# An attention block with an MLP: where row maxima are placed, who copies the sums, who normalizes the output rows, and how far maxima run ahead

## The chip, the core and the metric

The kernel runs on one core of a Trainium2 chip. The core has five engines that run side by side and meet only at semaphores: TensorE (PE in the profile, with its weight loads as PEld), VectorE (DVE), ScalarE (ACT), GpSimd (POOL) and SyncE (SP), which here only issues DMAs. Each engine takes its instructions strictly in the order in which they stand in its queue, so an instruction that waits holds up all that stand behind it. Matmul results land in PSUM, which has eight banks of 128 x 512 floats; everything else lies in SBUF or in DRAM. The metric is the device time of one execution in microseconds (us).

## The reference

Two pre-norm layers on a sequence of 2048 rows of 512 numbers, all in float32:

```
h  = x + softmax(q k^T / 4) v @ wo      with q, k, v = layernorm(x) @ wqkv, 32 heads of 16 columns
h2 = h + silu(layernorm(h) @ w1) @ w2   with 1792 hidden columns
```

The softmax is the exact one: each row's maximum over all 2048 keys is subtracted before the exponential.

## The kernel before

**Numbers.** Operands of most products are split into a high and a low half-precision part and multiplied in three products (high x high, low x high, high x low). Probabilities and values are multiplied in float32.

**Items and groups.** The attention works through 32 items; an item is one block of 512 query rows and four heads (`ITEMS`, eight items to a block of rows). An item has 16 groups; a group takes one chunk of 128 keys for the four heads. So there are 512 groups, g = 0 to 511, and c = g mod 16 is the place of a group in its item. A group consists of four score matmuls (`scores`, L469), four exponentials on ScalarE (`pt`, L480) and, one or two groups later, four matmuls of probabilities with values (`values`, L883), which add into one PSUM bank, `pv`, over the 16 groups of an item. A column of ones in the values gives the sums of the softmax.

**Maxima.** The exponent needs the row maximum before the scores are taken. So the scores are computed a second time, ahead: one matmul of 128 queries by 512 keys and one VectorE reduction (`maximum`, L292; the lines L308, and L306 where two heads go in one reduction). An item has 64 of these reductions. `maxima(g)` (L1376) says how many are done beside group g. When an item's last one is done (`found_maxima`, L405), `finish_max` folds them to 16 numbers on GpSimd and splits them into two half-precision rows (`ns`), and then one of two ways brings them into the query operand `qs` as two extra rows. `place_far` (L345) transposes on VectorE (`mt`), writes to DRAM (four DMAs, `md<-mt`) and reads back (two DMAs, `qs<-md`); it is called CALM groups later, or WAIT steps later before the attention starts. `place_max` (L358) transposes on TensorE, copies on VectorE (`mn`) and writes with two DMAs; it is for items that are found FAR groups or fewer before they start, and in that case GpSimd's folding is replaced by one VectorE reduction.

**Before the attention.** Layer norm, weight splits and projections run in a prologue of about 110 us, in blocks b = 0 to 3 of 512 rows. Beside each projection a few maxima of items 0 and 1 are done in pairs (`burst`). Which keys of item 0 may be used is in `at["loaded"]` (L772). After the blocks come three more query and key projections, and then group 0.

**Products beside groups.** In most groups the other work of TensorE is mixed in (`beside_products`, L1190): further query and key projections beside groups 0 to 115, and the MLP of the previous block of rows beside groups 146 to 257, 274 to 385 and 402 to 511. In such a group `maxima` gives four reductions, and five as long as fewer than 64 + 4 (g + LEAD) are done, though never past the end of the item that is being worked on. The groups between, 116 to 145, 258 to 273 and 386 to 401, have no product beside them. There the number comes from a rate that reaches the next items in time: four at most, three in many. These are the first item of a block and a little before and after it (`FIRSTS` = items 8, 16, 24; before item 8 also twelve groups of item 7).

**Output of a block.** In items 8, 16 and 24, groups c = 9 to 14, the previous block's attention output is projected with wo, four row tiles one after the other (`output`, L1236): in step n (c = 9 + n) TensorE's 12 matmuls and the sum with x of tile n, the split of tile n-2 into halves (`split_normal`, ScalarE's copy, then GpSimd's or for the last tile VectorE's subtraction), the layer norm of tile n-1 on VectorE (`normalize`, `hx<-ot`), and the statistics of tile n.

**End of an item.** `finish_item` (L901) copies `pv` to SBUF (`pvs`), the left half on ScalarE and the right half on VectorE, and starts the DMAs for the sums and the outputs. The last item's copy is followed by a tail of about 90 us, the last block's output and MLP.

**Order.** The engines' queues follow the order in which the program emits the instructions, with a few DMAs on SyncE interleaved differently where a memory pool is exchanged at group 124. Work for later is kept in an agenda by step, a step being a projection of the prologue or a group.

Of the kernel before, what the change touches and what calls it, by code (L numbers as in the profile page):

```python
# [10 lines left out]
F32 = mybir.dt.float32  # L11
# [3 lines left out]
AF = mybir.ActivationFunctionType  # L15
ALU = mybir.AluOpType
# [4 lines left out]
P = 128  # L21
# [43 lines left out]

WAIT = 2
AHEAD = 6
FAR = 8
CALM = 4


OUTPUT = 8

LOOK = 5

LEAD = 9


SWAP = 124
# [11 lines left out]
def attention_mlp_kernel(ctx: ExitStack, tc: tile.TileContext, x, wqkv, wo, w1, w2, out):  # L91
# [12 lines left out]
    def pool(op, *a, **k):  # L104
        tc.keep_in_program_order(getattr(nc.gpsimd, op)(*a, **k))  # L105
# [5 lines left out]
    def act(fn, *a, **k):  # L111
        ins = getattr(nc.scalar, fn)(*a, **k)  # L112
        pin(ins)
        return ins
# [6 lines left out]
    def dve(fn, *a, **k):  # L121
        pin(getattr(nc.vector, fn)(*a, **k))  # L122
# [110 lines left out]

    def normalize(dst, rows, mv, rs, engine="dve"):
        (pool if engine == "pool" else dve)("tensor_scalar", dst, rows, mv[:, 0:1], rs, op0=ALU.subtract, op1=ALU.mult)

    def turn(src, dst_h, dst_l, kind="st"):

# [142 lines left out]
    def soon(steps, fn, *a):  # L381

        agenda.setdefault(at["step"] + steps, []).append((fn, a))
# [21 lines left out]
    def found_maxima(piece):  # L405
        g = at["group"]
        if g is None or piece[1] is None and start_of(piece) - g > FAR:
            soon(WAIT if g is None else CALM, place_far, piece)
            finish_max(piece, False)
            return  # L410
        late.setdefault(at["step"] + WAIT, []).append(piece)
        unfinished.append(piece)
        found_at["step"] = at["step"]
# [348 lines left out]
    for b in range(NB):  # L762
        if b == 1:
            lay_out(sm=range(4), st=(7, 4, 5, 6))
        if b == NB - 1:
            lay_out(sm=range(6), st=[n for n in banks["st"] if n > 5])
        units = [("qk", 1, b), ("qk", 0, b) if b < 2 else ("qk", 3, b - 1)]
        vs = [("v", t, b) for t in range(4)]
        found = {}
        for n, (kind, k, of) in enumerate(units + vs if b else units):  # L770
            tick()
            at["loaded"] = b + (n > 3)  # L772
            square_rest(2 + 6 * (b - 1) + n if b else n)
            rows, (stats, norm, turns) = None, ((), (), ())
            if b + 1 < NB:
                rows = xts[b + 1]
                stats, norm, turns = (other_ln if b else first_ln)[n]
                if b == 2 and n < 4:
                    stats, norm = (((0, 1), (0,)), ((), (1,)), ((3,), (2,)), ((), ()))[n]

            def layer_norm():
                for of_norm in (kind == "v", kind != "v"):
                    for t in norm if of_norm else stats:
                        if of_norm:
                            normalize(rows[:, t, :], rows[:, t, :], *found.pop(t), engine="pool" if kind == "v" and (b, n) != (1, 2) else "dve")
                        else:
                            found[t] = statistics(rows[:, t, :], LN)

            if kind == "v":
                project_v(b, k)  # L790
            else:

                if (b, n) == (0, 1):
                    load_x(3)
                    for c in range(2):
                        pool("tensor_scalar", scaled[1 - c], raw_v[:, 2 + c], v_w, 1.0, op0=ALU.mult, op1=ALU.mult)
                    split_qk(splits.pop((b, n)))
                layer_norm()
                if (b, n) == (1, 0):
                    split_values(0)  # L800
                project_qk(of, k, scale=b > 0)
                if (b, n) == (0, 1):
                    split_values(1)
                if (b, n) in splits:
                    split_qk(splits.pop((b, n)))
                if n == 1:
                    for i in range(2):
                        for h in range(4):
                            if b == 0:
                                load_q(i, h)  # L810
                            load_k(i, h, b * 512, 512)
            if b:

                burst(BESIDE_V[b - 1][kind == "v"][n - 2 if kind == "v" else n])
            if (b, n) == (2, 0):
                stats, norm = (2,), ()
            if kind == "v" or (b, n) == (2, 0):
                layer_norm()
            if (b, n) == (2, 2):
                normalize(rows[:, 3, :], rows[:, 3, :], *found.pop(3), engine="pool")  # L820
            for t in turns:
                turn_x(b + 1, t)
            if b == NB - 1 and n < DC:
                split_x0(n)
            if (b, n) in splits:
                split_qk(splits.pop((b, n)), "pool")
            if b == 2 and n in (3, 5):
                fixed_rows(n // 4)
# [72 lines left out]
    def finish_item(i):  # L901

        b, u = divmod(i, 8)
        pvs = bp.tile([P, 512], F32, name="pvs", bufs=1)
        act("copy", pvs[:, :256], pv[:, :256])
        dve("tensor_copy", pvs[:, 256:], pv[:, 256:])
        if i == LAST:
            last.append(pvs)
            return
        dma(dn[i], pvs.rearrange("(k r) n -> k r n", r=32)[:, DH, :])  # L910
        for k in range(4):
            dma(ot[b % 2][place(i, k), :, u // 2, :], pvs[32 * k:32 * k + 16, :].rearrange("d (t n) -> d t n", n=P))

        steps = (1, 3, 4, 6) if u == 7 else (2, 6, 8, 10)
        for n, fn in zip(steps, (sums, invert, spread, divide) if u % 2 else (sums, invert, spread)):
            soon(n, fn, i)
        if i == ITEMS - 2:
            soon(10, divide_half)
            soon(12, split_half)
# [141 lines left out]
    def rows_of(b, t):  # L1061
        return ot[b % 2][:, t].rearrange("p c n -> p (c n)")
# [173 lines left out]
    def output(b, n):  # L1236

        if n < 4:
            ps = bank()
            run(project_rows(n, ps))  # L1240
            add_rows(b, n, ps)
        t = n - 3
        if t in halves:
            turn_beside(hts, slice(t * P, (t + 1) * P), halves.pop(t))
        t = n - 2
        if 0 <= t < 4:
            split_normal(t)
            if t == 3:
                turn_beside(hts, slice(t * P, (t + 1) * P), halves.pop(t))
        if 0 < n < 5:  # L1250
            normalize(hx[n - 1], rows_of(b, n - 1), *found.pop(n - 1))

        if n < 4:
            found[n] = statistics(rows_of(b, n), LN)
# [121 lines left out]
    def maxima(g):  # L1376
# [17 lines left out]
        at["due"] += rate  # L1394
        if g < LAG:
            return 0
        n = max(0, min(most, int(at["due"]), ready - at["done"]))
        at["due"] = min(4, at["due"] - n)
        return n
# [126 lines left out]
```

## Time and profile before

| | |
|---|---|
| median of three runs | 1618.02 us (1617.33 to 1620.47) |
| the profiled execution | 1617.63 us, of which the span from first to last instruction is 1615.9 us |
| PE busy | 1579.4 us, 98% |
| VectorE busy | 1380.6 us, 85%; 1211.8 of them 1956 reductions of single maxima |
| ScalarE busy | 1241.9 us, 77%; 1068.2 of them 2048 exponentials |
| GpSimd busy | 580.2 us, 36% |
| mean granted TensorE clock | 0.996 |

PE's busy time is no measure of how full PE is, since matmuls overlap; what counts is the distance from one group to the next. Rows of a timeline give the start and the time taken by a run of like instructions (x4 means four), and in square brackets how long the engine had been idle before it and what it waited for. The chain of waits gives the pieces of work that set the end, in order of time. In a row of stretches, an engine's busy time is followed by its number of instructions in brackets, and the columns after POOL are the granted TensorE clock, the DMA share and GB/s.

### The profile page before, as it was taken

What the parts mean: (1) busy time and instruction counts of PE and PEld (TensorE: products, weight loads), DVE (VectorE), ACT (ScalarE), POOL (GpSimd) and SP (SyncE); (2) the same over time, 40 slices, a digit from 0 to 9 for tenths busy, and PEclk for the clock granted to TensorE, in tenths of its full rate; (3) what the DMA queues carried; (4) which work ended last, traced back from release to release, by engine and by line L of the source; (5) the groups of instructions that cost most, each with busy time, mean ns of one, the idle gap of its engine ahead of it and who ended that gap; (6) DMA issues with size and microseconds to landing.
All of it is one profiled execution on the core that took longest, in us unless ns stands there. A gap on an engine that the chain in (4) does not pass through costs nothing.

```text
span 1615.9 us, 31905 instructions
## 1 busy us (share of the span) xinstructions
PE 1579.4 (98%) x11735; PEld 488.3 (30%) x11735; DVE 1380.6 (85%) x2279; ACT 1241.9 (77%) x2412; POOL 580.2 (36%) x875
## 2 busy tenths in 40 slices
PE   9979999999999999999999999999999999999999
PEld 6422233333222222222222222222222222222354
DVE  7979999999988999999989999999989999991232
ACT  5548988888876888877777888877767888878632
POOL 6631255645522444412143445311143444311100
PEclk9989999999999999999999999999999999999999
DMA  6653334444433122344424222444433122434322
GB/s 219 163 139 95 106 84 125 131 122 131 126 77 84 43 59 59 90 142 144 117 57 96 51 50 53 118 136 124 114 93 66 45 59 59 119 103 139 121 84 74
DMA packets 135993, 162.23 MB, mean 100 GB/s; under 512 B 43248, under 2 KB 79856, under 8 KB 135836
## 3 DMA queue, kind: packets, MB, share of 16 engines
q1 hardware_dynamic: 133388, 155.86, 34.6%
q10 hardware_dynamic: 2448, 4.33, 1.0%
q8 instruction: 92, 1.51, 0.4%
q14 instruction: 65, 0.53, 0.1%
HBM read 126.71 MB, written 24.85 MB: 94 GB/s over the span
## 4 chain that ended last, share of the span: by engine, by line
PE 83%; DVE 9%; ACT 3%; POOL 2%; issue 2%; DMA 1%; SPq 0%; POOLq 0%; ACTq 0%
PE ps L98 82%; DVE mx L308 6%; ACT pt L112 2%; DVE mx L306 1%; DVE pvs L122 1%; POOL w L105 1%; ACT pvs L112 1%; PE ps L101 1%; DVE st L122 0%; DVE hx L122 0%; SPq L128 0%; DMA qs<-md 0%; POOL sl L105 0%; DMA ot<-in_A_wo_dram 0%; ACT sh L112 0%
## 5 line engine op out<-in xcount | busy, mean ns | idle before, releaser
L308 DVE TENSOR_REDUCE mx<-ps 128x1 f32<-128x512 f32 x1956 | 1211.8, 682 | 72.8 <-PE ps L98 68.2
L112 ACT ACTIVATE pt<-ps 128x512 f32<-128x512 f32 x2048 | 1068.2, 604 | 252.7 <-PE ps L98 247.7
L98 PE MATMUL ps<-qs,ks 64*128 64x512 f16 x2048 | 736.6, 380 | 10.1 <-DMA qs<-md 8.8
L98 PE MATMUL ps<-ks,qs 48*128 48x512 f16 x2048 | 675.2, 380 | 19.0 <-DVE mx L308 10.7
L98 PE MATMUL ps<-pt,va 128*17 128x512 f32 x4096 | 545.1, 598 | 0.0
L98 PE MATMUL ps<-hts,w 64*128 64x512 f16 (+2 forms) x1212 | 285.7, 370 | 0.0
L98 PEld LDWEIGHTS <-qs 48*128 48x128 f16 x2048 | 156.6, 94 | 388.1 <-issue 367.7
L98 PE MATMUL ps<-w,gates 64*128 64x512 f16 x1008 | 246.4, 376 | 0.6
L98 PEld LDWEIGHTS <-ks 64*128 64x128 f16 x2048 | 186.4, 94 | 97.7 <-issue 86.1
L105 POOL TENSOR_TENSOR ri<-rc,minus 128x16 f32<-128x16 f32 x31 | 90.8, 2928 | 195.2 <-DMA rc<-dn 195.2
L98 PEld LDWEIGHTS <-w 64*128 64x128 f16 (+1 forms) x1212 | 114.4, 95 | 134.1 <-issue 36.8
L98 PEld LDWEIGHTS ps<-pt,va 128*17 128x17 f32 x4096 | 73.7, 95 | 222.6 <-issue 218.8
L98 PEld LDWEIGHTS <-gates 64*128 64x128 f16 x1008 | 92.8, 94 | 132.0 <-issue 32.0
L105 POOL TENSOR_SCALAR t<-t,factors 128x512 f32<-128x512 f32 x42 | 29.0, 691 | 187.1 <-ACT t L112 187.1
L112 ACT ACTIVATE g<-ps,factors 128x512 f32<-128x512 f32 x68 | 47.3, 696 | 43.7 <-PE ps L98 42.7
L105 POOL TENSOR_TENSOR sl<-scaled,sh 128x512 f16<-128x512 f32 x30 | 34.7, 1156 | 127.3 <-ACT sh L112 117.5
L98 PE MATMUL ps<-xth,wqk_h 64*128 64x512 f16 (+1 forms) x204 | 77.8, 382 | 0.0
L98 PE MATMUL ps<-xth,wqk_l 64*128 64x512 f16 (+1 forms) x204 | 77.7, 381 | 0.0
L98 PE MATMUL ps<-xtl,wqk_h 64*128 64x512 f16 (+1 forms) x204 | 77.5, 380 | 0.0
L105 POOL TENSOR_TENSOR ot<-ot,g 128x512 f32<-128x512 f32 x12 | 15.2, 1266 | 172.9 <-ACT g L112 172.9
L122 DVE COPY pvs<-ps 128x256 f32<-128x256 f32 (+1 forms) x33 | 14.3, 432 | 56.2 <-ACT pvs L112 39.1
L306 DVE TENSOR_REDUCE mx<-ps 128x2 f32<-128x1024 f32 x46 | 53.3, 1217 | 3.7 <-PE ps L98 3.5
(163 smaller groups left out, 1038.8 us busy)
## 6 DMA issues: line engine op xcount, KB each, us to landing
w<-w2d SPq DMA_DIRECT2D x182, 256.0 KB
ks<-kd SPq DMA_DIRECT2D x120, 192.0 KB
w<-w1d SPq DMA_DIRECT2D x56, 256.0 KB
w<-in_B_w_dram SPq DMA_DIRECT2D x28, 256.0 KB
qs<-qd SPq DMA_DIRECT2D x128, 48.0 KB
kd<-sh SPq DMA_DIRECT2D x16, 256.0 KB
qd<-sh SPq DMA_DIRECT2D x16, 256.0 KB
junk<-in_B_w_dram ACTq DMA_DIRECT2D x16, 256.0 KB
```

Source lines behind the costliest of these rows:

```text
L98: return tc.keep_in_program_order(nc.tensor.matmul(*a, **k))
L101: tc.keep_in_program_order(nc.tensor.transpose(*a))
L105: tc.keep_in_program_order(getattr(nc.gpsimd, op)(*a, **k))
L112: ins = getattr(nc.scalar, fn)(*a, **k)
L122: pin(getattr(nc.vector, fn)(*a, **k))
L306: pin(nc.vector.tensor_reduce(of, space[:, n:n + 2, :], axis=AX.X, op=ALU.max))
L308: pin(nc.vector.tensor_reduce(of[:, j:j + 1], space[:, n, :], axis=AX.X, op=ALU.max))
```

## The change

Four things change. In the prologue, the keys of a block count as loaded one projection sooner, and an item found before the attention is placed one step later instead of two. During the attention FAR goes from 8 to 5 and CALM from 4 to 3. The sums `pv` are copied by ScalarE in one instruction for every item but the last. In `output`, the rows are normalized by ScalarE with a bias that GpSimd works out first. And LEAD goes from 9 to 7, while in groups c = 9 to 15 of the items in `FIRSTS` the full number of maxima is taken as long as fewer than 64 + 4 (g + LEAD + 4) are done.

```
-FAR = 8
-CALM = 4
+FAR = 5
+CALM = 3
...
-LEAD = 9
+LEAD = 7
...
+    def normalize_act(dst, rows, mv, rs):
+        shift = small.tile([P, 1], F32, name="shift", bufs=4)
+        pool("tensor_scalar", shift, mv[:, 0:1], rs, -1.0, op0=ALU.mult, op1=ALU.mult)
+        act("activation", dst, rows, AF.Identity, bias=shift, scale=rs)
...
     def found_maxima(piece):
         g = at["group"]
         if g is None or piece[1] is None and start_of(piece) - g > FAR:
-            soon(WAIT if g is None else CALM, place_far, piece)
+            soon(1 if g is None else CALM, place_far, piece)
...
-            at["loaded"] = b + (n > 3)
+            at["loaded"] = b + (n > 2)
...
     def finish_item(i):
         b, u = divmod(i, 8)
         pvs = bp.tile([P, 512], F32, name="pvs", bufs=1)
-        act("copy", pvs[:, :256], pv[:, :256])
-        dve("tensor_copy", pvs[:, 256:], pv[:, 256:])
+        if i == LAST:
+            act("copy", pvs[:, :256], pv[:, :256])
+            dve("tensor_copy", pvs[:, 256:], pv[:, 256:])
+        else:
+            act("copy", pvs, pv)
...
     def output(b, n):
...
         if 0 < n < 5:
-            normalize(hx[n - 1], rows_of(b, n - 1), *found.pop(n - 1))
+            normalize_act(hx[n - 1], rows_of(b, n - 1), *found.pop(n - 1))
...
     def maxima(g):
...
+        if i in FIRSTS and c > OUTPUT and 64 + 4 * (g + LEAD + 4) > at["done"]:
+            at["due"] = max(at["due"], most)
         n = max(0, min(most, int(at["due"]), ready - at["done"]))
```

## The prediction

> **What bounds the kernel now.** I read the page first, then the chain of waits, then VectorE's timeline, and last the spots where PE waits.
>
> ```profile
> PE 1579.4 (98%) x11735; PEld 488.3 (30%) x11735; DVE 1380.6 (85%) x2279; ACT 1241.9 (77%) x2412; POOL 580.2 (36%) x875
> ...
> PE 83%; DVE 9%; ACT 3%; POOL 2%; issue 2%; DMA 1%; SPq 0%; POOLq 0%; ACTq 0%
> ```
>
> PE sets the end for most of the span, so a saving on another engine counts only where that engine comes onto the chain. VectorE does so at three kinds of places. The first is the end of an item; VectorE's timeline shows it in item 13:
>
> ```profile
> 722.83 2.48 DVE L308 TENSOR_REDUCE mx<-ps 128x1 f32<-128x512 f32 x4 [0.19 <-PE ps L98]
> 725.62 0.42 DVE L122 COPY pvs<-ps 128x256 f32<-128x256 f32 x1 [0.31 <-ACT pvs L112]
> 725.96 2.47 DVE L308 TENSOR_REDUCE mx<-ps 128x1 f32<-128x512 f32 x4
> ```
>
> VectorE waits for ScalarE's half of the copy, then copies its own; from one group's reductions to the next it is 3.13 us (725.96 - 722.83), where an ordinary group with MLP products and four maxima takes 2.67 (rows below, where the 0.19 in brackets shows VectorE waiting for PE). So its reductions start 0.46 late. The chain of waits, at an earlier item, runs through both copies and back to PE:
>
> ```profile
> 595.52 0.38 ACT pvs L112
> ...
> 595.92 0.42 DVE pvs L122
> ...
> 597.00 3.05 PE ps L98 x23
> ```
>
> The second is a group with five maxima; the third, the groups without products:
>
> ```profile
> 526.82 9.19 DVE L308 TENSOR_REDUCE mx<-ps 128x1 f32<-128x512 f32 x15 [0.48 <-PE ps L98]
> ...
> 541.73 2.49 DVE L308 TENSOR_REDUCE mx<-ps 128x1 f32<-128x512 f32 x4 [0.19 <-PE ps L98]
> 544.40 2.48 DVE L308 TENSOR_REDUCE mx<-ps 128x1 f32<-128x512 f32 x4 [0.19 <-PE ps L98]
> ```
>
> Fifteen back to back are three groups of five: 9.19 / 3 = 3.06 us, 0.38 more than a group of four (544.40 - 541.73 = 2.67). Without products, PE's matmuls of probabilities with values mark the groups:
>
> ```profile
> 440.53 1.05 PE L98 MATMUL ps<-pt,va 128*17 128x512 f32 x8
> 443.02 1.05 PE L98 MATMUL ps<-pt,va 128*17 128x512 f32 x8
> 445.03 1.05 PE L98 MATMUL ps<-pt,va 128*17 128x512 f32 x8
> ```
>
> The first distance, 2.49 us, is a group with four maxima, VectorE's pace; the second, 2.01, one with three. Maxima are therefore not free there: a fourth costs 0.48.
>
> **A. The start.**
>
> ```profile
> 96.81 0.24 POOL L105 TENSOR_TENSOR mx<-mx 128x32 f32<-128x32 f32 x1 [7.43 <-DVE mx L306]
> ...
> 99.41 0.22 POOL L105 TENSOR_TENSOR ns<-nm,ns 128x16 f16<-128x16 f32 x1
> ...
> 101.17 0.20 DVE L122 STREAM_TRANSPOSE mt<-ns 128x32 f16<-128x32 f16 x1
> 101.30 3.45 DVE L306 TENSOR_REDUCE mx<-ps 128x2 f32<-128x1024 f32 x3
> ...
> 104.80 0.49 PE L98 MATMUL ps<-ks,qs 48*128 48x512 f16 x1 [2.12 <-DVE mx L306]
> ...
> 105.64 2.33 SPq L128 DMA_DIRECT2D md<-mt  x4
> ...
> 106.31 0.15 DVE L122 TENSOR_SCALAR factors<-norms 128x1 f32<-128x1 f32 x1 [1.56 <-POOL norms L105]
> ...
> 112.68 0.58 PE L98 MATMUL ps<-qs,ks 64*128 64x512 f16 x1 [7.39 <-DMA qs<-md]
> ```
>
> Item 0's last maximum ends at 96.8, but its rows land at 112.7, because placing comes two steps later and the four writes stand on SP behind the stores of a projection. In the burst plan, loading one projection sooner brings item 0's last pair forward by three paired reductions (3.45 us, the row of x3), to 93.3. GpSimd's folding takes 2.8 (96.81 to 99.63), so `ns` is ready at 96.1, and the step that places it now comes two projections sooner. One transpose, four writes and two reads then stand ahead of the stores of two projections on SP. The rows land 7.0 after the writes start (105.64 to 112.68), so near 103.5. The stores behind them wait some 5 us, and behind those the key loads of item 2, wanted only from group 9 on. VectorE pays: the transpose now stands before nine paired reductions. VectorE reaches it at 94.3 (six reductions of 1.15 before 101.2) and waits until 96.1, so the nine end 1.8 later, at 106.6 instead of 104.75, and PE, which already waits for them at 104.80, starts the first scores near 106.8 instead of 112.68. GpSimd's `norms`, behind a projection that is 2 later, hold VectorE's first single maximum until 109.
>
> ```profile
> 117.08 0.48 DVE L122 MEMSET ps<- 128x512 f32 x1
> ...
> 119.13 1.05 PE L98 MATMUL ps<-pt,va 128*17 128x512 f32 x8
> ```
>
> From there two groups of four maxima at 0.61 and the memset take 5.4 us, to 114.4, and the first values stand about 1 us before the last of them, near 113.3 against 119.1: **-5.8**. Bounds: -9.5, both PE waits gone (7.39 + 2.12); and 0, if the key blocks wanted one projection sooner land late.
>
> ```profile
> 112.68:119.00 6.32, 6.32 (x29) 2.18 (x28) 4.68 (x8) 4.14 (x7) 0.00 (x0) 0.53 0.61 165
> 119.00:135.00 16.00, 15.89 (x124) 4.43 (x123) 15.94 (x27) 13.02 (x28) 1.16 (x1) 1.00 0.22 64
> ```
>
> These stretches show the granted clock at 0.53 after the long wait and 1.00 later. The Trainium skill (TensorE: Matmul & The Clock Gate, "What's actually happening") says that the array falls to half clock after an idle window of about 3.4 us and needs as long to come back. By that rule a wait of 2 us keeps full clock and A holds; if 4 us remain, the slow stretch stays and A is nearer -3.
>
> **B. One copy instead of two.** VectorE's copy and its wait go; ScalarE takes 0.61 for all 512 columns (row below) instead of 0.38, so its next exponentials start 0.23 later.
>
> ```profile
> L112 ACT ACTIVATE scaled<-ps 128x512 f32<-128x512 f32 x30 | 18.4, 614 | 18.1 <-PE ps L98 11.6 <-POOL sl L105 3.6 <-POOL xtl L105 2.6
> L112 ACT ACTIVATE g<-ps,factors 128x512 f32<-128x512 f32 x68 | 47.3, 696 | 43.7 <-PE ps L98 42.7
> ```
>
> The cover is that only a group's fourth score needs a bank back, the first one's (three are in use), and by then the first exponential has just ended even 0.23 later; where it hasn't, PE waits up to 0.23. Ten ends beside the MLP's second product get 0.41 each (4.1). At nine ends beside its first product, ScalarE also has `g` (0.70) in that group, and the product whose bank `g` reads waits an estimated 0.2: 0.25 each (2.25). Seven beside projections give 0.25 (1.8), four without products 0.45 (1.8); the last gives nothing. Sum **-10.0**. Bounds: -14 (31 x 0.46), and -4 if ScalarE's 0.23 and `g` reach PE everywhere.
>
> **C. Fewer groups of five.** Working through `maxima(g)` for both settings gives the counts of fives: item 0, 11 and none; item 9, 9 and 4; item 17, 9 and 2; items 25 and 26, 14 and 4. The item-end rule cuts one group to a single maximum in item 0, which then takes four. Beside the MLP a five saves 0.38: 1.9, 2.4 (after 0.3 for a group of two that becomes four) and 3.7. In item 0, nine are left outside A; I take 0.3 each, 2.7, less than 0.38 because ScalarE also has its squares there. Sum **-10.7**, between -8 and -12.5 (33 x 0.38).
>
> **D. The groups without products.** The same work moves there. Ten groups outside the output steps go from three to four (+4.8), three go from four to three (-1.4). In output steps VectorE's normalize goes:
>
> ```profile
> 846.48 0.54 DVE L122 TENSOR_SCALAR hx<-ot,mv,rs 128x512 f32<-128x512 f32 x1
> ...
> 848.46 0.37 PE L98 MATMUL ps<-ks,qs 48*128 48x512 f16 x1 [0.79 <-DVE mx L308]
> ```
>
> The fourth maximum's matmul waits 0.79 for a bank; 0.54 of that goes where there were four already, while threes become fours. Over the twelve steps c = 9 to 12 I take -1.0. Together **+2.4**, between 0 and +5.
>
> **E. ScalarE behind GpSimd at c = 13.** Here I expect a new wait.
>
> ```profile
> 852.87 2.06 ACT L112 ACTIVATE pt<-ps 128x512 f32<-128x512 f32 x4 [3.25 <-PE ps L98]
> 854.79 0.64 ACT L112 CAST g<-hx 128x512 f16<-128x512 f32 x1
> 855.30 2.10 ACT L112 ACTIVATE pt<-ps 128x512 f32<-128x512 f32 x4
> 857.22 0.68 ACT L112 CAST g<-hx 128x512 f16<-128x512 f32 x1
> ```
>
> ```profile
> 855.50 1.37 POOL L105 TENSOR_TENSOR g<-hx,g 128x512 f16<-128x512 f32 x1 [0.94 <-ACT g L112]
> ```
>
> ```profile
> 853.56 1.85 DVE L308 TENSOR_REDUCE mx<-ps 128x1 f32<-128x512 f32 x3
> ...
> 858.18 0.68 DVE L122 TENSOR_TENSOR g<-hx,g 128x512 f16<-128x512 f32 x1
> ```
>
> In each output step ScalarE's cast of tile n-2 is followed on GpSimd by a subtraction (1.37), and only behind that stands the new bias. ScalarE's normalization waits for it, and the next group's exponentials stand behind. With two operands per row I take it at 0.78 (0.614 with none, 0.696 with one). At c = 10 to 12 the 12 matmuls cover this (ScalarE idles 3.25 at 852.87). At c = 13 there are none: the cast ends at 855.43, the bias near 857.2, the normalization near 858.0, against exponentials now at 855.30. The last cast moves from 857.22 to 860, and VectorE's last subtraction, which waits for it, from 858.18 to 860.7, two us after VectorE runs dry even with four maxima in each group. The subtraction and four reductions then end near 863.9, so groups 13 to 15 take 10.3 us from 853.56. Now VectorE's work there is 11, 9 and 9 reductions (by the rate rule) at 0.62, a normalization of 0.54 and the subtraction: 8.0, 6.8 and 6.8. The difference is 2.3 + 3.5 + 3.5, less 0.3 for waits that are there already: **+9.0**. Bounds: +2.5, VectorE's own work alone (12 reductions and the subtraction, 8.1), and +12.
>
> **Placing with LEAD 7.** Items are found eight groups ahead instead of ten and placed five instead of six, 13.3 us.
>
> From the transpose it takes about 7.2 (0.2, then the 7.0 of A): hidden. Items 8, 9, 17 and 25 have four groups of 2.49, about 10, and item 8 waits already:
>
> ```profile
> 449.43 0.39 PE L98 MATMUL ps<-qs,ks 64*128 64x512 f16 x1 [1.39 <-DMA qs<-md]
> ```
>
> Its placing moves one group later, and what stands before it on SP moves too; I take no change. Items 9, 25 and 26 lose `place_max`, a small reduction and a copy on VectorE each: -0.3 in all.
>
> **The sum.** -5.8 - 10.0 - 10.7 + 2.4 + 9.0 - 0.3 = -15.4. The profiled execution took 1617.63 (span 1615.9), 0.4 below the median of 1618.02. 1617.6 - 15.4 gives 1602.2: **1602**.
>
> **Rivals.**
> 1. E is absorbed, because groups 13 to 15 start with ScalarE ahead: 6.5 less, 1596. For it: 77% busy. Against it: the chain cast, subtraction, bias, normalization is serial. 0.20.
> 2. ScalarE takes VectorE's place at item ends: B is -4, 1608. For it: it sums 0.61 + 2.06 + 0.70 = 3.4 us in a group of 2.67. Against it: only nine ends have `g`. 0.14.
> 3. The start gains about 1, because key blocks land late or VectorE's wait grows: 1607. 0.08.
> 4. Placing is late at the four items without products ahead, 2 us each: 1610. For it: item 8's 1.39 and a queue on SP that other stores hold up. Against it: 7.2 against 10. 0.08.
> 5. Slower: the normalization's function isn't in ScalarE's loaded table, so each of the 12 needs two loads. It decides from seven onwards (7 x 2 x 1.28 = 17.9). All 12 cost 30.8: 1632. Against it: the page's rows show two loads in all. 0.05.
>
> ```profile
> L112 ACT ACT_TABLE_LOAD x2 | 2.6, 1283 | 0.7 <-PEq L1512 0.7
> ```
>
> The Trainium skill (ScalarE: Activation LUTs, "Table sets: the hidden batching unit") speaks against rival 5: cheap functions, identity among them, are in every set. The row agrees for copies, squares and tanh; no run here shows the identity yet.
>
> 6. The change doesn't bring what it moves: 2 and 4 together (+14) leave 1616, and E at its upper end 1619. 0.05.
>
> **How the numbers follow.** The forecast has 0.40. The range 1592 to 1612 takes in rivals 1 to 4, the upper bound of E, and A or B at their better ends; rivals 5 and 6 and a few stray cases stay out. About 0.2%, 3.2 us, is what a measurement of this kernel can tell from no change. Faster is the forecast and rivals 1 to 4: 0.90. The same is rival 6: 0.05. Slower is rival 5: 0.05.
>
> **What would show it.** A: PE's first score near 107, clock 1.00 behind it; 112 is wrong. B: at item ends 2.67 to 2.9 between groups, no VectorE copy; 3.1 is wrong. C: fives only in items 9, 17 and 25. D and E: groups at 2.49, and ScalarE idle before each normalization, waiting for GpSimd; 8.5 us over c = 13 to 15 refutes E. Placing: no PE wait for `qs<-md` over 2 us. The whole is wrong if a wait that I don't name takes over 10 us.

## The result and the profile after

The changed kernel takes 1615.15 us (median of 8 runs, 1613.47 to 1616.23) beside 1618.16 of the kernel before (1617.29 to 1621.47): a ratio of 0.9976, interval 0.9966 to 0.9987. It is faster by 3.0 us, where 16 were forecast, and 3 us outside the predicted range. Its profiled execution has a span of 1612.3 us, 3.6 less than before. Of the four executions of the kernel with three repairs, further below, one ran at a granted clock of 0.75 and took 1904.4 us; its median of 1600.7 counts that one, and the other three alone have 1600.3.

First the page of the changed kernel, engines and chain:

```profile
PE 1574.8 (98%) x11732; PEld 486.2 (30%) x11732; DVE 1365.5 (85%) x2233; ACT 1254.3 (78%) x2424; POOL 589.3 (37%) x905
...
PE 84%; DVE 7%; ACT 4%; DMA 2%; POOL 2%; issue 1%; SPq 0%; POOLq 0%; ACTq 0%; DVEq 0%
PE ps L98 83%; DVE mx L313 6%; ACT pt L112 2%; DMA hts<-g 1%; PE ps L101 1%; DMA kd<-sl 1%; DVE st L122 0%; POOL g L105 0%; DVE mx L311 0%; DVE ot L122 0%; ACT g L112 0%; ACT sh L112 0%; DMA ks<-kd 0%; POOL sl L105 0%; SPq L128 0%
```

VectorE's share of the chain falls from 9% to 7%. Two DMAs, `hts<-g` and `kd<-sl`, have 1% each: these two lead to most of what the prediction lacked.

To see where the 3.6 us come from, I take the start of each group's value matmuls on PE and look at the distances. Steps 13 to 16 below means the stretch from the value matmuls that stand at the end of step c = 12 to those at the end of the next item's first step, summed over items 8, 16 and 24; steps 3 to 12 is the stretch before it.

| us | before | after | difference |
|---|---|---|---|
| first value matmul | 119.1 | 116.1 | -3.0 |
| item 0 | 47.3 | 45.4 | -1.8 |
| items 1 to 7 | 289.5 | 288.6 | -0.9 |
| items 9, 17, 25, 26 | 178.7 | 168.8 | -9.8 |
| items 10 to 15, 18 to 23, 27 to 29 | 649.1 | 642.7 | -6.4 |
| items 8, 16, 24: steps 3 to 12 | 110.8 | 114.8 | +4.0 |
| items 8, 16, 24: steps 13 to 16 | 30.4 | 45.9 | **+15.5** |
| items 8, 16, 24: the two steps after | 18.0 | 16.7 | -1.3 |
| item 30 | 41.9 | 42.3 | +0.4 |

They add up to -3.3. All the gains are there; one short stretch, three times, takes back most of them.

**The gains.** VectorE and ScalarE at the end of an item beside MLP products (timeline of the changed kernel):

```profile
717.97 2.48 DVE L313 TENSOR_REDUCE mx<-ps 128x1 f32<-128x512 f32 x4 [0.19 <-PE ps L98]
720.64 2.48 DVE L313 TENSOR_REDUCE mx<-ps 128x1 f32<-128x512 f32 x4 [0.19 <-PE ps L98]
723.37 1.29 DVE L313 TENSOR_REDUCE mx<-ps 128x1 f32<-128x512 f32 x2 [0.25 <-PE ps L98]
...
720.36 0.59 ACT L112 COPY pvs<-ps 128x512 f32<-128x512 f32 x1 [0.29 <-PE ps L98]
```

VectorE's copy is gone; the next group's reductions start after 2.67 and 2.73 us instead of 3.13, and ScalarE's copy takes 0.59. The fives, in item 9:

```profile
510.53 11.64 DVE L313 TENSOR_REDUCE mx<-ps 128x1 f32<-128x512 f32 x19 [0.83 <-PE ps L98]
522.36 2.48 DVE L313 TENSOR_REDUCE mx<-ps 128x1 f32<-128x512 f32 x4 [0.19 <-PE ps L98]
```

Nineteen are three fives and a four, and then fours with slack for VectorE.

**The loss.** ScalarE, GpSimd, SyncE and PE at c = 12 to 16 of item 16, from timelines of the changed kernel:

```profile
843.28 1.70 SPq L128 DMA_DIRECT2D md<-mt  x4
846.12 0.52 SPq L128 DMA_DIRECT2D qs<-md  x2
...
847.50 1.30 SPq L132 DMA_TRANSPOSE hts<-g  x1
...
851.01 0.62 ACT L112 CAST g<-hx 128x512 f16<-128x512 f32 x1 [0.66 <-DMA hts<-g]
853.27 0.81 ACT L112 ACTIVATE hx<-ot,shift,rs 128x512 f32<-128x512 f32 x1 [1.64 <-POOL shift L105]
...
851.71 1.16 POOL L105 TENSOR_TENSOR g<-hx,g 128x512 f16<-128x512 f32 x1 [2.06 <-ACT g L112]
852.97 0.27 POOL L105 TENSOR_SCALAR shift<-mv,rs 128x1 f32<-128x1 f32 x1
...
846.88 1.05 PE L98 MATMUL ps<-pt,va 128*17 128x512 f32 x8
...
854.62 0.41 PE L98 MATMUL ps<-qs,ks 64*128 64x512 f16 x1 [1.41 <-ACT pt L112]
...
857.97 0.58 PE L98 MATMUL ps<-ks,qs 48*128 48x512 f16 x1 [1.30 <-DVE mx L313]
...
861.92 1.05 PE L98 MATMUL ps<-pt,va 128*17 128x512 f32 x8
```

The same place before:

```profile
842.05 1.70 SPq L128 DMA_DIRECT2D md<-mt  x4
...
846.65 1.31 SPq L132 DMA_TRANSPOSE hts<-g  x1
...
851.46 1.05 PE L98 MATMUL ps<-pt,va 128*17 128x512 f32 x8
...
861.05 1.05 PE L98 MATMUL ps<-pt,va 128*17 128x512 f32 x8
```

The stretch is 15.0 us (846.88 to 861.92) instead of 9.6. ScalarE's normalization waits 1.64 us for the bias, which stands on GpSimd behind the subtraction of another tile: that is the wait of term E. But the subtraction itself starts late, because ScalarE's cast of this tile waited 0.66 us for a buffer, which a transposing transfer was still reading. That transfer comes late in its group: before, the first one is issued 4.8 us ahead of the stretch (846.65 against 851.46); after, 0.6 us behind its start (847.50 against 846.88). On SP it stands behind the placing of the next item, which now falls into the same step, and whose two reads are issued 2.84 us behind its first write. Last, PE's clock falls. Stretches of the changed kernel (the column behind POOL is the granted clock):

```profile
852.15:854.62 2.47, 1.06 (x10) 0.23 (x10) 1.44 (x3) 1.35 (x3) 0.99 (x2) 1.00 1.34 90
854.62:857.97 3.35, 2.00 (x8) 0.47 (x7) 1.34 (x3) 3.35 (x8) 0.00 (x0) 0.53 0.78 197
857.97:861.57 3.60, 3.60 (x15) 0.59 (x15) 1.92 (x4) 1.14 (x4) 0.00 (x0) 0.50 0.75 180
```

The first step after the waits takes 3.4 to 3.7 us in the three items, at a clock of 0.50 to 0.54, where it took 2.5 to 2.8 at full clock. How much of this is the clock no run shows by itself.

### The profile page after: what moved, and what is told of

Read it like the earlier page. It is cut to its first block, busy times and chain, and to the rows that moved or that the text cites. A ratio compares the mean times of both kernels' runs of the same rounds, so it can differ in the third digit from the quotient of the medians.

```text
span 1612.3 us, 31826 instructions
## 1 busy us (share of the span) xinstructions
PE 1574.8 (98%) x11732; PEld 486.2 (30%) x11732; DVE 1365.5 (85%) x2233; ACT 1254.3 (78%) x2424; POOL 589.3 (37%) x905
## 3 DMA queue, kind: packets, MB, share of 16 engines
q1 hardware_dynamic: 133880, 155.89, 34.9%
## 4 chain that ended last, share of the span: by engine, by line
PE 84%; DVE 7%; ACT 4%; DMA 2%; POOL 2%; issue 1%; SPq 0%; POOLq 0%; ACTq 0%; DVEq 0%
PE ps L98 83%; DVE mx L313 6%; ACT pt L112 2%; DMA hts<-g 1%; PE ps L101 1%; DMA kd<-sl 1%; DVE st L122 0%; POOL g L105 0%; DVE mx L311 0%; DVE ot L122 0%; ACT g L112 0%; ACT sh L112 0%; DMA ks<-kd 0%; POOL sl L105 0%; SPq L128 0%
## 5 line engine op out<-in xcount | busy, mean ns | idle before, releaser
L98 PE MATMUL ps<-ks,qs 48*128 48x512 f16 x2048 | 676.0, 381 | 22.0 <-DVE mx L313 13.3
L105 POOL TENSOR_TENSOR t<-t,g 128x512 f32<-128x512 f32 x42 | 53.6, 1277 | 3.5
```

The source lines that it names most:

```text
L98: return tc.keep_in_program_order(nc.tensor.matmul(*a, **k))
```

## The experiments

All medians, with the ratio to the kernel before in the same comparison and its interval; the two stretches are the sums defined above. A stretch comes from the one profiled execution of its kernel, which can lie some us from the median (1596.7 beside 1600.7 with three repairs).

| kernel | median us | ratio | steps 3 to 12 | steps 13 to 16 |
|---|---|---|---|---|
| before | 1618.2 to 1619.3 | | 110.8 | 30.4 |
| after | 1615.2 | 0.9976 (0.9966 to 0.9987) | 114.8 | 45.9 |
| after, VectorE normalizes | 1609.3 | 0.9932 (0.9915 to 0.9948) | 116.8 | 38.0 |
| after, bias a step earlier | 1610.2 | 0.9945 (0.9928 to 0.9962) | 114.8 | 39.6 |
| after, three buffers | 1611.1 | 0.9956 (0.9942 to 0.9970) | 114.8 | 39.8 |
| after, both | 1602.9 | 0.9896 (0.9879 to 0.9912) | 114.8 | 32.6 |
| after, CALM 2 | 1616.5 | 0.9988 (0.9978 to 0.9997) | 114.8 | 42.0 |
| after, norm earlier | 1611.9 | 0.9959 (0.9945 to 0.9973) | 114.8 | 46.4 |
| before + one copy | 1610.2 | 0.9951 (0.9935 to 0.9968) | 111.7 | 30.4 |
| before + constants | 1617.0 | 0.9991 (0.9982 to 1.0001) | 114.6 | 34.9 |
| before + normalization | 1623.9 | 1.0029 (1.0016 to 1.0042) | 109.2 | 37.1 |
| before + start | 1616.0 | 0.9983 (0.9974 to 0.9993) | 110.8 | 30.4 |
| after + three repairs | 1600.7 | 0.9885 (0.9866 to 0.9905) | 114.9 | 32.5 |
| the same, VectorE normalizes | 1603.2 | 0.9905 (0.9889 to 0.9922) | 116.8 | 34.2 |
| the same, without the rule | 1598.2 | 0.9875 (0.9858 to 0.9892) | 113.7 | 31.4 |
| the same, LEAD 9 | 1603.5 | 0.9904 (0.9887 to 0.9920) | 111.1 | 32.3 |

### VectorE normalizes again

```
-            normalize_act(hx[n - 1], rows_of(b, n - 1), *found.pop(n - 1))
+            normalize(hx[n - 1], rows_of(b, n - 1), *found.pop(n - 1))
```

> The changed kernel with one part undone: the twelve rows of the output steps are normalized by VectorE again. What is compared is the time of groups 13 to 16 of items 8, 16 and 24, by the distances between PE's value matmuls: 30.4 us in the kernel before, 45.9 in the changed one. Theory: the new wait of ScalarE for GpSimd's bias costs nearly all of these 15.5 us. Then the stretch falls to 31 to 34 us here (VectorE's 0.54 per row comes back), and the median lies near 1602 (1615.2 less 12 to 15). Rival: the stretch is slow because more maxima were moved into it by the earlier placing. Then it stays above 42 us and the median within 3 us of 1615.

The stretch falls to 38.0 us, and the median by 5.8. Neither theory holds: about half of the 15.5 goes, and half stays although ScalarE waits for no bias. The view of waits of this kernel names what stays (us in all, times, longest):

```profile
ACT g L112 <- DMA hts<-g: 5.1, 6, 1.7
```

ScalarE's casts wait for the transposing transfers, here longer than in the changed kernel.

### The bias a step earlier, three buffers, and both

GpSimd computes the bias right behind the statistics of its row:

```
+    def shift_of(mv, rs):
+        shift = small.tile([P, 1], F32, name="shift", bufs=4)
+        pool("tensor_scalar", shift, mv[:, 0:1], rs, -1.0, op0=ALU.mult, op1=ALU.mult)
+        return shift, rs
...
-            found[n] = statistics(rows_of(b, n), LN)
+            found[n] = shift_of(*statistics(rows_of(b, n), LN))
```

> The changed kernel, but GpSimd works out the bias right behind the row's statistics, a group earlier, so that it no longer stands behind the subtraction of another tile; ScalarE still normalizes. Theory of two links (GpSimd's order holds ScalarE for 1.63 us, the buffer of the halves that a transposing transfer still reads for 0.79): groups 13 to 16 of the three items fall from 45.9 to about 40 us (1.63 less at each, and what the lower clock behind it cost), median near 1609. Rival A, GpSimd's order alone: below 36 us and below 1606. Rival B, the buffer alone: 44 us or more, median above 1613.

And the halves have a ring of three of their own:

```
-        rows, halves[t] = hx.pop(t), parts_of(zp.tile([P, 512], F32, name="g"))
+        rows, halves[t] = hx.pop(t), parts_of(zp.tile([P, 512], F32, name="g3", bufs=3))
```

> The changed kernel, but the fp16 halves of the normalized rows have three buffers of their own instead of sharing two, so that the cast needs no buffer that a transposing transfer still reads. GpSimd's order is as in the changed kernel. Theory of two links: groups 13 to 16 of the three items fall by 0.8 us at each, from 45.9 to about 43, median near 1612.5. Rival A, GpSimd's order alone: 45 us or more, median within 1 us of 1615. Rival B, the buffer alone: below 38 us, median below 1608.

> The changed kernel with both: the bias a group earlier, and three buffers for the halves. Theory of two links: neither wait is left, groups 13 to 16 of the three items take 31 to 35 us, as in the kernel before, and the median lies at 1600 to 1605, not above that of the kernel with VectorE's normalization. Rival: ScalarE's own work (the normalization of 0.81 us, four exponentials of 2.06 and a cast of 0.62 to 0.68 in one group) is the bound there: the stretch stays above 38 us and the median above 1608.

The waits of the changed kernel have both causes:

```profile
ACT hx L112 <- POOL shift L105: 21.4, 12, 2.2
...
ACT g L112 <- DMA hts<-g: 2.4, 3, 1.0
```

With the bias earlier only the second is left:

```profile
ACT g L112 <- DMA hts<-g: 4.3, 5, 1.6
```

With three buffers only the first is left, unchanged (21.4 us, 12 times). With both edits neither row is there, and the same stretch of item 16 takes 10.8 us:

```profile
843.98 1.05 PE L98 MATMUL ps<-pt,va 128*17 128x512 f32 x8
...
852.55 0.37 PE L98 MATMUL ps<-ks,qs 48*128 48x512 f16 x1 [1.21 <-DVE mx L316]
...
854.81 1.05 PE L98 MATMUL ps<-pt,va 128*17 128x512 f32 x8
```

The bias is worth 6.3 us in the three stretches (45.9 to 39.6), the buffers 6.1, both together 13.3. The theory of two links holds, also in the medians (4.9, 4.0 and 12.3). The third buffer is worth twice what its 0.8 us of wait had led me to expect; part of it is the first step of the next item, which gets 1.7 and 1.0 us shorter in items 8 and 24, where the granted clock is 1.00 and 0.75 instead of 0.50 and 0.53.

### Placing one step earlier

```
-CALM = 3
+CALM = 2
```

> The changed kernel with one constant changed: an item's maxima are placed two steps after they are found (CALM 2) instead of three. New theory: the loss in groups 13 to 16 begins on SP. In the changed kernel the four writes and two reads of the placing stand on SP just ahead of the first transposing transfer, which is issued 22.4 us behind the value matmuls of group 8 instead of 16.9 (the reads wait on SP for the writes). So the transfers land late, the two buffers of the halves come free late, and ScalarE's cast waits. With the placing one step earlier the transfers are issued near 17 again. Then no cast waits for a transfer, GpSimd's order alone is left, groups 13 to 16 of the three items take 34 to 38 us (45.9 in the changed kernel) and the median is 1603 to 1607. Rival: the casts wait whatever the place of the placing, because three transfers of 1.25 us of issue and 3.5 us of landing need more than two buffers: the stretch stays above 42 us and the median above 1612.

SyncE of this kernel, item 16, whose stretch begins at 850.0:

```profile
840.92 1.70 SPq L128 DMA_DIRECT2D md<-mt  x4
...
845.61 1.30 SPq L132 DMA_TRANSPOSE hts<-g  x1
```

The first transfer is issued 4.4 us ahead of the stretch again, and no cast waits for one, so the late transfers do come from the placing on SP. But GpSimd's order alone then costs more than I had expected: 42.0 us, not 34 to 38. The figures are those of the rival, its mechanism is not, since no cast waits. Of the 2.2 us more than with three buffers, 2.0 lie in the first step of the next item (10.0 us against 8.0 in the three items), where the granted clock is 0.52 to 0.60 here and 0.53, 0.75 and 1.00 there, behind the same waits for the bias; why it falls further here is left open. And the edit has a price elsewhere that I had not seen. The waits of this kernel:

```profile
DVE mt L122 <- POOL ns L105: 8.4, 23, 1.8
```

VectorE's transpose now comes before GpSimd has folded the maxima, in 23 items; in the changed kernel such a wait is there once, at the start. Item 0 gets 1.2 us longer, items 2 to 6 get 0.5, most others 0.15. So the median is no better, 1616.5.

### The constants alone

```
-FAR = 8
-CALM = 4
+FAR = 5
+CALM = 3
...
-LEAD = 9
+LEAD = 7
```

> The kernel before with the three constants alone: maxima seven groups ahead, placed from five groups, three steps after they are found; VectorE still normalizes and copies its half. By the prediction's terms the fewer groups of five save about 10 us (nearly all of -10.7) and the groups without products cost up to 3: about 1611. Theory of SP's order: the placing stands ahead of the first transposing transfer here too, so groups 13 to 16 of items 8, 16 and 24 take 36 to 40 us instead of 30.4 although ScalarE does not normalize, and the median is 1615 to 1619. Rival: without ScalarE's wait for GpSimd the late transfers cost nothing: below 33 us and 1609 to 1613.

Items 0, 9, 17, 25 and 26 are 9.7 us shorter in all, as term C says (-10.7). Steps 3 to 12 cost 3.8 more and steps 13 to 16 4.5 more (34.9, a little below the expected 36), though VectorE normalizes and the clock stays at 1.00 there. The waits of this kernel:

```profile
ACT g L112 <- DMA hts<-g: 5.1, 6, 2.0
```

The kernel before has no such row. So the three constants bring the late transfers by themselves. The median is 1.7 us lower, which its interval does not tell from nothing.

### The normalization alone

It is the kernel before with `normalize_act` and its call in `output` as in the change.

> The kernel before with one part of the change: ScalarE normalizes the rows of the output steps, with the bias from GpSimd. The transposing transfers are issued as early as in the kernel before. Theory of two causes: GpSimd's order alone costs what term E said, 9 us or a little more in groups 13 to 16 of items 8, 16 and 24 (30.4 to 39 to 42 us), the output steps ahead of them lose VectorE's 0.54 per row (about 2 us less), no cast waits over 0.3 us for a transposing transfer, and the median is 5 to 9 us above that of the kernel before. Rival: the two buffers hold the casts here too, and the stretch takes 44 us or more, as in the changed kernel (10 us or more slower). Second rival: without the maxima moved there ScalarE has room, and the stretch stays below 35 us.

The median is 5.0 us above the kernel before; the stretch is 37.1, 6.7 more, and steps 3 to 12 are 1.6 shorter. The wait that it adds is the one for the bias, and no cast waits for a transfer:

```profile
ACT hx L112 <- POOL shift L105: 21.4, 12, 2.2
```

By itself this part of the change makes the kernel slower. The stretch costs less than the 9 to 12 expected; fewer maxima stand in it than in the changed kernel, which may be why. The start, the copy, the constants and the normalization run alone add up to -8.1 us (-2.9, -8.5, -1.7 and +5.0, with the two below), and the whole change gives -3.0. In the stretch the constants alone cost 4.5 and the normalization alone 6.7, together 11.2, and the whole change 15.5: there the late transfers and the wait for the bias seem to cost more together than each by itself. But the whole change also has the new rule of `maxima`, which was not run alone on the kernel before, so the difference is not all shown to be theirs.

### One copy alone

It is the kernel before with `finish_item` as in the change.

> The kernel before with one part of the change: an item's sums are copied by ScalarE alone. The prediction gives -10.0 us for this part, between -14 and -4; the two traces side by side give about -9.6. Then the median is 1608 to 1609 with 1618.2 before, and an item's end beside MLP products takes 2.67 to 2.75 us instead of 3.12. Rival: ScalarE is the bound at the ends (its 0.23 us and the sigmoid's share reach PE): 1612 to 1614.

The median is 8.5 us lower; by the profile the last item starts 7.9 us sooner. An end beside the MLP takes 2.67 to 2.73.

### The start alone, and with the norm earlier

The start alone is the kernel before with these two lines:

```
-            soon(WAIT if g is None else CALM, place_far, piece)
+            soon(1 if g is None else CALM, place_far, piece)
...
-            at["loaded"] = b + (n > 3)
+            at["loaded"] = b + (n > 2)
```

> The kernel before with the start alone: one projection's key blocks counted as loaded sooner, and maxima found ahead of the attention placed one step later instead of two. Theory: the first value matmul moves from 119.1 to about 116 us as in the changed kernel, with GpSimd's norm still behind the store of the low halves, and the median falls by 2 to 4 us. Rival: what starts sooner waits later for the keys of items 1 and 2 or for the squares of ScalarE, and the median stays within 1.5 us of the kernel before.

The first value matmul is at 116.5 and the median falls by 2.9, as the theory says. In the profiled execution (1617.4 us) most of this is lost again at the end of item 7: PE waits 2.1 us there for placed rows (1.39 before), the clock falls behind it, and item 7 takes 43.9 us instead of 41.6. The rival had named other waits.

Why not 113? The chain of waits of the changed kernel, up to PE's second wait:

```profile
103.60 0.78 POOL sl L105
104.38 3.80 DMA kd<-sl
...
108.34 1.16 POOL sl L105
...
109.90 0.58 POOL norms L105
...
110.51 0.16 DVE factors L122
...
111.05 0.60 DVE mx L313
...
111.69 1.02 PE ps L98 x3
```

The low half `sl` has two buffers; GpSimd's third waits for the store of an earlier one, which is issued on SP at 104.38, behind the placing and the fixed rows. Behind that subtraction stands GpSimd's norm, behind the norm VectorE's factors, and behind these its single maxima. To take the norm out of this chain, its two GpSimd operations were moved ahead of the last block's projections:

```
+    def output_norm():
         pool("tensor_scalar", norms[:, 3:], norms[:, 3:], 1e-30, None, op0=ALU.add)
         pool("tensor_tensor", norms[:, 3:], norms[:, 3:], expos[:, 3:], ALU.pow)
+
+    def set_output_factors():
         scale_of(slice(3, 4), TOP / BOUND)
...
             lay_out(sm=range(6), st=[n for n in banks["st"] if n > 5])
+            output_norm()
```

> The changed kernel, but GpSimd's two small operations on the output weights' norm run before the last block's projections, not behind the last three. Theory: at the start VectorE's factors, and behind them its first single maxima, wait 2.69 us for this norm, which stands on GpSimd behind a subtraction that waits 3.58 us for a store of the low halves; the store stands on SP behind the placing. Then VectorE's first single maximum starts near 108.3 us instead of 110.97, PE's wait of 2.36 us at 111.69 goes, the first value matmul stands at 113 to 114 (116.1 in the changed kernel), and the median falls by 2 to 3 us, to 1612 to 1613. Rival: another wait holds PE there, the scores' bank or the keys: the first value matmul stays within 0.7 us of 116 and the median at 1615.

VectorE and PE of this kernel:

```profile
107.60 0.15 DVE L122 TENSOR_SCALAR factors<-norms 128x1 f32<-128x1 f32 x1
...
108.15 2.48 DVE L313 TENSOR_REDUCE mx<-ps 128x1 f32<-128x512 f32 x4
...
107.74 0.37 PE L98 MATMUL ps<-ks,qs 48*128 48x512 f16 x1 [2.03 <-DVE factors L122]
...
112.34 1.05 PE L98 MATMUL ps<-pt,va 128*17 128x512 f32 x8
```

And its stretch behind PE's wait, where the changed kernel has its low clock:

```profile
107.80:112.30 4.50, 3.89 (x28) 1.31 (x27) 4.34 (x10) 3.64 (x7) 1.54 (x3) 1.00 0.85 164
```

The factors no longer wait, the 2.36 us of PE's second wait are gone, the clock stays at 1.00, and the first value matmul is at 112.3. The median is 3.3 us lower than that of the changed kernel.

### Three repairs together, and what the parts are worth then

This is the changed kernel with the earlier bias, the three buffers and the earlier norm.

> The changed kernel with three repairs: the bias worked out a group earlier, three buffers of their own for the halves, and the norm of the output weights ahead of the last projections. If the places are independent, the first two give 12.3 us (1602.9 against 1615.2) and the third 3.3 (1611.9 against 1615.2): 1599.6, with groups 13 to 16 of items 8, 16 and 24 at 32 to 33 us and the first value matmul at 112 to 113. Rival: part of the gain at the start only moves a wait (an item found earlier waits for its keys): 1601 or more.

1600.7 us, 14.4 below the changed kernel, where the repairs one by one give 12.3 and 3.3: they add up to within 1.2 us. Three variants of it:

> The same as the kernel with three repairs, but VectorE normalizes the rows of the output steps. It tells what moving the normalization is worth once the buffers don't hold. Theory: with VectorE's normalization alone put back, groups 13 to 16 still took 38 us because the casts waited for transposing transfers; with three buffers they take 32 to 34 here, groups 3 to 12 take 2 us more than with ScalarE, and the median is 1600 to 1603. Rival: the rows on VectorE hold the stretch: 36 us or more, and 1604 or more.

> The kernel with three repairs without the new rule that puts four maxima into the output steps' groups. Theory (the same maxima cost about the same elsewhere): the output steps of items 16 and 24 get about 2 us shorter, and items 17 and 25, where fives come back, 1.2 longer; the median stays within 1.5 us of the kernel with three repairs. Rival: the rule is needed, since late maxima come back as groups of five or as a late placing: 3 us or more slower.

The rule is the one in `maxima` for the items in `FIRSTS`.

> The kernel with three repairs, but with maxima nine groups ahead and the placing as in the kernel before (LEAD 9, FAR 8, CALM 4). Theory: fewer groups of five are worth 9.8 us (items 0, 9, 17, 25 and 26), and what they cost in items 7, 8, 16 and 24 is 4 to 8 us once ScalarE's waits are gone, so the seven groups pay 2 to 6 us: 1602 to 1606 here. Rival: moving the maxima is worth nothing by itself, because a fourth maximum without products costs 0.48 us and a fifth beside products 0.38: 1597 to 1601.

VectorE's normalization costs 1.9 us in steps 3 to 12 and 1.7 in steps 13 to 16; the medians differ by 2.5, with intervals that overlap. So by the traces ScalarE's normalization pays, once nothing holds it, and the medians fit that without showing it. Without the rule the median is 1598.2, 2.5 lower where at most 1.5 was expected, but its interval does not tell it from the kernel with the rule. With nine groups ahead again the median is 2.8 us more, again with overlapping intervals: that the seven groups pay about that is likely, not shown. The kernel with three repairs beats both kernels of this case, the one before by 18.6 us and the changed one by 14.4; the one without the rule does so by 21.1 and 16.9.

## Why the prediction was wrong, point by point

| term | predicted | measured |
|---|---|---|
| A, the start | -5.8 | -3.0 |
| B, one copy | -10.0 | -8.5 alone |
| C, fewer fives | -10.7 | -9.7 (constants alone) |
| D, groups without products | +2.4 | +4.0 in steps 3 to 12, some 0.8 of it from B |
| E, ScalarE behind GpSimd | +9.0 | +15.5 in its stretch |
| placing | -0.3 | not measured alone; no wait of PE for placed rows is left |

Of the 12.4 us between the forecast sum (-15.4) and the median's -3.0, E's stretch has 6.5 and A 2.8; B, C and D have 1.0 to 1.6 each. (Together this is 13.4, since some of B's loss is counted in D again.)

**E, and the placing in front of it.** The mechanism is right, and where only the wait for the bias is left its size is about right too: the stretch is then 6.7 (normalization alone), 9.4 (three buffers) or 11.6 us (CALM 2) longer than before. What failed is the step "Its placing moves one group later, and what stands before it on SP moves too; I take no change." I had looked at whether PE waits for the placed rows, and not at what stands behind them on SP. Behind them stands the first transposing transfer; it came 5.4 us later against the stretch (4.8 ahead, 0.6 behind), held one of two buffers, and a cast of ScalarE, GpSimd's subtraction, the bias and the exponentials followed. It is worth 6 to 7 us (45.9 to 39.8, and 39.6 to 32.6 with the bias earlier). E had taken the casts at the times of before, "the cast ends at 855.43". E also had no term for the clock, which fell to about half behind these waits in all three items. Of the bounds, +12 was too low; the lower one, +2.5 for VectorE's own work, is what is left when both links are broken (32.6 against 30.4).

**A.** The first score of item 0 no longer waits 7.39 us for its rows, as forecast. The step that failed is "GpSimd's `norms`, behind a projection that is 2 later, hold VectorE's first single maximum until 109": it was 110.97. The store on SP, and not the projection, held it, because the placing had moved ahead of it. PE of the changed kernel then waited twice:

```profile
107.87 0.37 PE L98 MATMUL ps<-ks,qs 48*128 48x512 f16 x1 [2.03 <-DVE mx L311]
...
111.69 0.58 PE L98 MATMUL ps<-ks,qs 48*128 48x512 f16 x1 [2.36 <-DVE mx L313]
```

and its clock fell to 0.50 during the second wait and stayed there in the stretch behind it:

```profile
111.70:116.10 4.40, 4.14 (x21) 1.13 (x24) 4.27 (x8) 2.28 (x4) 0.00 (x0) 0.50 0.87 265
```

The prediction had written what this would make of A: if some 4 us of waiting remain, "A is nearer -3". Two waits of 2.03 and 2.36 us remained, and A was -3.0; with only the 2.03 left the clock stayed at 1.00. So both cases came out as the prediction had drawn them from the rule of the Trainium skill (TensorE: Matmul & The Clock Gate, "What's actually happening"). But that rule asks for an idle window of about 3.4 us, and no wait at this place was that long in these two kernels: the reason is not the one it gives (last section). In the kernel before, too, the clock fell at 104.92, behind PE's wait of 2.12 us and ahead of the long one of 7.39.

**B and C** are right, 1.5 and 1 us smaller. In B, ends beside the MLP's first product gain 0.4, more than the 0.25 taken; of the ends beside projections most gain 0.2 to 0.4, but with one copy alone item 4's loses 0.3 and those of items 0 and 1 lose 0.2 and 0.5. At item 0's end PE then waits 0.71 us for ScalarE's exponentials, where it waited 0.17 before: ScalarE is the later one there. And steps 3 to 8 of items 8, 16 and 24 get 0.8 longer with one copy alone.

**D** was mis-sized in its second part. Steps 3 to 8 of the three items take 4.1 us more (45.4 to 49.5), but 0.8 of this comes with the one copy, and with the constants alone it is 3.3, where 3.4 were counted. Steps 9 to 12 take the same as before (65.4 and 65.3), where -1.0 was taken. VectorE's time for the rows did come back there: with VectorE normalizing again they take 67.3. But threes had become fours, and without the new rule, in the kernel with three repairs, they take 1.1 less (64.2 against 65.3).

**The rivals.** Rival 5, table loads, did not happen; the changed kernel has the two loads of before:

```profile
L112 ACT ACT_TABLE_LOAD x2 | 2.6, 1283 | 0.7 <-PEq L1522 0.7
```

That is what the Trainium skill says (ScalarE: Activation LUTs, "Table sets: the hidden batching unit"), and it now rests on a row: identity needed no load. Rival 4, placing late, did not happen in the profiled run of the changed kernel: no wait of PE for `qs<-md` is left there. The wait at the end of item 7 (1.39 before) stands, at 1.4 to 2.1 us, in the profiled executions of all five kernels with the old placing, and with the new one in two of eleven (both edits, 2.1; three repairs without the rule, 1.6). So placing with LEAD 7 did change something, mostly for the better. The time came out where rival 6 stood, but of its parts only E at its upper end, and beyond it, came true: neither the copies nor PE's wait for placed rows had a part in it.

## What to carry to other kernels

When a step moves on an in-order DMA queue, follow not only what it brings but what stands behind it: here six small DMAs, moved by a step, made a transposing transfer late, and with two buffers that came back through four engines. A ring of two buffers whose reader is a DMA had no slack in time here; look for the row "engine waits for DMA" on the writer of that buffer. Put small operations that another engine waits for (a bias, a norm) behind their inputs, not behind large ones whose order doesn't matter.

## What the runs showed of the hardware

PE's clock fell where no single wait was longer than 1.41 us: in item 16 PE waited 1.41 us, and at the end of this wait, at 854.83, the granted clock fell to 0.50. (The second wait there, 1.30, comes after the fall.) But PE also waited 1.39 us in the kernel before (at 449.43), and the clock stayed:

```profile
448.03:449.43 1.40, 0.01 (x3) 0.01 (x1) 0.33 (x1) 0.47 (x1) 0.00 (x0) 1.00 0.98 189
449.43:451.50 2.07, 2.07 (x17) 0.64 (x19) 1.56 (x3) 1.65 (x4) 0.00 (x0) 1.00 0.76 287
```

It stayed with the earlier norm behind 2.03 us too. And at the end of item 7 it fell behind a wait of 2.06 us with the start alone, and stayed behind one of 2.08 in the kernel with both edits. So the length of one wait doesn't decide. The traces show something of what does: in each of them the clock changes only at points of a grid of 3.41 us, and the low stretches last 3.41 us or a whole multiple of it (6.83 in item 16). This is the grid there, in the changed kernel:

```profile
851.42:854.83 3.41, 1.89 (x14) 0.34 (x11) 2.17 (x4) 1.77 (x4) 1.43 (x2) 1.00 1.27 131
854.83:858.24 3.41, 2.06 (x8) 0.36 (x5) 1.61 (x3) 3.41 (x8) 0.00 (x0) 0.50 0.69 176
...
861.66:865.07 3.41, 3.25 (x27) 0.61 (x24) 3.32 (x6) 3.10 (x7) 0.00 (x0) 1.00 0.06 16
```

In the 3.41 us ahead of each of the 29 falls in the sixteen traces (between 80 and 1560 us), PE was busy for 0.37 to 1.90 us. Of the 6851 other such stretches at full clock, all but five have 1.93 or more; those five have 1.53 to 1.91. So sparse work within one stretch of the grid goes with the fall. It also seems to matter where a wait lies on the grid: the 2.06 us at the end of item 7 lay within one stretch (444.03 to 447.44) and left PE busy for 1.4 us of it, while the 2.08 and the 2.03 were cut in two by a point of the grid (at 445.20 and 107.26) and left 1.80 and 1.86, two of the five. The Trainium skill (the page and section named above) puts the window at about 3.4 us, which agrees with the grid, but of idleness; the rows of item 16 show a fall with 1.89 of 3.41 us busy, and the measurement decides. What exactly the clock counts is not settled: in the five exceptions it stayed, at 1.53 us busy in one of them.
